# A fixed order for the first four token tiles of a linear-attention and gated-MLP kernel on Trainium2

## The chip, the cores and the metric

The kernel runs on one core of one Trainium2 chip. The metric is the device time of one execution in microseconds (us), as the median of several runs. Before the change it is 2445.57 us, the median of 3 runs (2445.08 to 2446.03).

## What is computed

The input x has 2048 tokens of 1024 features, all in float32. The tokens are layer-normalized, and two branches work on the result xn. Branch A is linear attention with 32 heads of 32 features; branch B is a gated MLP with 3584 hidden features. The result is `x + A * silu(B)`.

```python
xn = layernorm(x)                                   # over the 1024 features, eps 1e-5
q, k, v = split_heads(xn @ wqkv)                    # 32 heads of 32
phi = lambda p: concat(softmax(p), softmax(-p))     # p = q @ w_phi or k @ w_phi, per head
kv, z = phi(k).T @ v, sum(phi(k))                   # per head, over all tokens
o = (phi(q) @ kv) / (phi(q) @ z + 1e-6)
A = merge_heads(o) @ wo
B = (sigmoid(xn @ w_gate) * (xn @ w_up)) @ w_down
out = x + A * silu(B)
```

## The kernel before

**Products.** Every large product is computed by Strassen's scheme in the form of Winograd: seven block products (named B11, B21, T2, T3, T4, T1, B22) in place of eight, with sums of blocks ahead of and behind them. To keep float32 accuracy, each operand is split into a high half in a rounded format (ScalarE's cast at L123) and the rest (VectorE's subtraction at L124); `mm3` adds three products, high by high (L128), high by low (L129) and low by high (L130).

**Tokens and weights.** The tokens are worked on in two halves (c = 0, 1) of eight tiles of 128 tokens. For each half the kernel projects to V, K and Q, each in the order B11, B21, T2, T3, T4, T1, B22, and then does the MLP's gate and up products. One block product of a projection runs over four token groups u, and for each over four k blocks with three matrix instructions each, so 12 matrix instructions for a group and 48 for a product. Operands of weights are kept in a ring of eight slots, filled by `prep()` (a cast and a subtraction of 128x1024 elements, for two slots).

**The opening.** A tile is loaded (`x_load`, L150), normalized (`norm`) and transposed by TensorE in two halves of four 128x128 transposes (`transpose`, L192), into one of four banks of PSUM (banks 4 to 7) that are used in turn. The normalization takes statistics on VectorE (two instructions at L160 and one at L161), adds eps (L165, GpSimd for the first half of the tokens), takes a root on ScalarE (L166) and the reciprocal on VectorE (L167), corrects it by five or six small steps on GpSimd (L169 to L174) and applies scale and bias on ScalarE (L176). Group u of B11 and B21 needs tile u, so tiles 0 to 3 are needed first; a transposed tile is split at once for these two (`operand`), and copied to SBUF by ScalarE (L196) for the sums that later blocks need. T2 and all that follows need sums of tiles 0 to 3 with tiles 4 to 7 (`x_sums`, L204). The sums of V's weight blocks (`v_sums`, L255) are made in place on VectorE and GpSimd once the four blocks have landed; those of K and Q follow from folding w_phi into the weights on TensorE (`fold`, L273), copies by ScalarE (L274), four sums on GpSimd (L229 to L232) and stores to DRAM (L224).

**What sets the order.** The program is traced in the order of the Python code. The framework then orders each engine's instructions, and the DMA issues on SP's queue, by a simulated schedule in which what was traced first has priority among what is ready; `tc.high_priority()` raises a block, and `tc.issue_after(ins)` lets a block come behind `ins` on its engine. Each engine then works strictly in that order. The work on the tiles is put between the groups' products by the list `side`, from which `step()` takes one entry behind each group. In the version before, tile 0 comes first with high priority, then all the `prep()` that fits, then the entries tile 1; tiles 2 and 3; tiles 4 and 5; `v_sums`; tiles 6 and 7; folds.

## Time and profile before

| | us |
|---|---|
| median of 3 runs | 2445.57 |
| the profiled execution | 2443.43 |
| its span, from the first to the last instruction | 2441.6 |
| TensorE busy | 2392.8 |
| VectorE busy | 1716.9 |
| ScalarE busy | 1001.9 |
| GpSimd busy | 987.2 |

The profile shows one execution. In it PE is TensorE's matrix work and PEld its weight loads, DVE is VectorE, ACT is ScalarE, POOL is GpSimd and SP is the engine that issues the loads and stores. A row of the timeline gives the start and the duration of an instruction (or of several alike, xN) in us from the span's start, engine, line, what it writes and reads, and, where the engine had been idle, for how long and what ended that. Durations of instructions that follow each other on an engine overlap a little. In a table by stages each engine has its busy time and its count of instructions; the granted clock of TensorE is a share of full speed.

### The profile page before, as it was taken

The numbers are of one execution on the slowest core, as the hardware profiler recorded it, in microseconds if no ns is written. First come the engines' busy times: TensorE is split into PE (matmuls) and PEld (weight loads), VectorE is DVE, ScalarE is ACT, GpSimd is POOL, SyncE is SP. The second block draws the span as 40 slices with busy tenths as digits, with TensorE's granted clock in tenths as the row PEclk, the third lists the DMA queues.
The fourth block names the chain that finished last, engine by engine and source line by source line (L and its number), as shares of the span: only waits on it lengthen the run. The fifth ranks groups of instructions, "written<-read, shape, count | busy, mean of one in ns | idle before, by whom it ended". The sixth has DMA issues, their size and how long they took to land.

```text
span 2441.6 us, 31984 instructions
## 1 busy us (share of the span) xinstructions
PE 2392.8 (98%) x11076; PEld 1986.7 (81%) x11076; DVE 1716.9 (70%) x2247; ACT 1001.9 (41%) x1495; POOL 987.2 (40%) x665
## 2 busy tenths in 40 slices
PE   7999999999999999999999999999999999998998
PEld 6888888888888878888888888788888888877886
DVE  6533577777776678548858888647889998765554
ACT  6432244544444344323433444423443334454332
POOL 5520146566565400004545453543333335314554
PEclk8999999999999999999999999999999999999999
DMA  7874567777776665457888887896666766755553
GB/s 280 279 255 157 195 226 261 255 257 271 263 276 242 245 216 174 172 203 249 292 301 284 275 316 257 278 339 216 217 231 219 254 218 238 236 197 191 182 182 128
DMA packets 231507, 581.61 MB, mean 238 GB/s; under 512 B 30385, under 2 KB 30385, under 8 KB 226737
## 3 DMA queue, kind: packets, MB, share of 16 engines
q1 hardware_dynamic: 231344, 579.57, 68.7%
q8 instruction: 87, 1.43, 0.2%
q14 instruction: 76, 0.61, 0.1%
HBM read 353.76 MB, written 225.71 MB: 237 GB/s over the span
## 4 chain that ended last, share of the span: by engine, by line
PE 77%; DMA 7%; DVE 6%; issue 4%; POOL 4%; ACT 2%; SPq 0%; ACTq 0%; POOLq 0%; DVEq 0%
PE bank L128 25%; PE bank L130 25%; PE bank L129 25%; DVE x L124 1%; DMA fc<-wf_d 1%; DMA w<-ws_d 1%; PE bank L448 1%; DMA fa<-w_down 1%; PE bank L627 1%; DVE w L124 1%; DMA fb<-w_down 1%; DVE p L124 1%; DMA fb<-wo 1%; ACT x L123 1%; DMA fc<-xo_d 0%
## 5 line engine op out<-in xcount | busy, mean ns | idle before, releaser
L128 PE MATMUL bank<-x,w 128*128 128x512 f32 x2352 | 912.7, 390 | 5.1 <-DVE fb L833 3.1
L129 PE MATMUL bank<-x,w 128*128 128x512 f32 x2352 | 915.9, 389 | 0.5 <-DVE x L124 0.4
L130 PE MATMUL bank<-x,w 128*128 128x512 f32 x2352 | 906.7, 389 | 0.0
L123 ACT CAST w<-fa 128x512 fp32r<-128x512 f32 (+1 forms) x444 | 308.2, 698 | 560.3 <-PE bank L129 335.8
L124 DVE TENSOR_TENSOR w<-fa,w 128x512 fp32r<-128x512 f32 (+1 forms) x444 | 434.8, 984 | 140.7 <-ACT w L123 134.1
L128 PEld LDWEIGHTS bank<-x,w 128*128 128x128 f32 x2352 | 441.6, 188 | 98.6 <-DVE fb L833 4.4
L130 PEld LDWEIGHTS bank<-x,w 128*128 128x128 f32 x2352 | 441.6, 188 | 91.9 <-DVE w L124 0.4
L129 PEld LDWEIGHTS bank<-x,w 128*128 128x128 f32 x2352 | 441.7, 188 | 91.2 <-DVE x L124 1.2
L128 PE MATMUL bank<-w,x 128*128 128x512 f32 x708 | 279.2, 394 | 3.7 <-ACT fb L384 2.1
L130 PE MATMUL bank<-w,x 128*128 128x512 f32 x708 | 278.5, 394 | 1.8 <-DVE x L124 1.8
L129 PE MATMUL bank<-w,x 128*128 128x512 f32 x708 | 277.9, 393 | 0.0
L841 POOL TENSOR_TENSOR fc<-fc 128x512 f32<-128x512 f32 x27 | 43.6, 1615 | 298.9 <-DVE fc L840 286.8
L128 PEld LDWEIGHTS bank<-w,x 128*128 128x128 f32 x708 | 134.0, 189 | 31.8 <-ACT fb L384 2.5
L130 PEld LDWEIGHTS bank<-w,x 128*128 128x128 f32 x708 | 133.8, 189 | 30.0 <-DVE x L124 2.5
L129 PEld LDWEIGHTS bank<-w,x 128*128 128x128 f32 x708 | 134.0, 189 | 27.2 <-DVE w L124 0.2
L577 POOL TENSOR_TENSOR fc<-fc 128x1024 f32<-128x1024 f32 x32 | 81.4, 2543 | 178.3 <-ACT fc L413 123.1
L841 POOL TENSOR_TENSOR fb<-fb,fc 128x512 f32<-128x512 f32 x57 | 91.2, 1600 | 130.7 <-DVE fc L840 107.3
L317 POOL TENSOR_TENSOR fb<-fa 128x512 f32<-128x512 f32 x28 | 36.7, 1309 | 248.2 <-DMA fa<-w_gu 133.7
L124 DVE TENSOR_TENSOR w<-fb,w 128x512 fp32r<-128x512 f32 (+1 forms) x114 | 106.0, 929 | 39.2 <-ACT w L123 37.7
L123 ACT CAST w<-fb 128x512 fp32r<-128x512 f32 (+1 forms) x114 | 71.4, 627 | 133.6 <-PE bank L129 103.8
L124 DVE TENSOR_TENSOR x<-fa,x 128x512 fp32r<-128x512 f32 x112 | 111.1, 993 | 15.6 <-ACT x L123 15.3
L840 DVE TENSOR_TENSOR fc<-fc,bank 128x512 f32<-128x512 f32 x84 | 57.3, 683 | 89.8 <-PE bank L130 75.8
(250 smaller groups left out, 3312.2 us busy)
## 6 DMA issues: line engine op xcount, KB each, us to landing
ws_d<-w SPq DMA_DIRECT2D x112, 512.0 KB, 3.9
w<-ws_d SPq DMA_DIRECT2D x112, 512.0 KB, 5.4
fa<-w_gu SPq DMA_DIRECT2D x84, 512.0 KB, 4.2
fa<-h_d SPq DMA_DIRECT2D x84, 512.0 KB, 4.1
fa<-wf_d SPq DMA_DIRECT2D x32, 1024.0 KB, 5.3
h_d<-fc SPq DMA_DIRECT2D x120, 256.0 KB, 4.0
fc<-e_d SPq DMA_DIRECT2D x48, 512.0 KB, 3.9
fc<-qkv_d SPq DMA_DIRECT2D x80, 256.0 KB, 4.2
```

Of the source, the lines that this page charges most:

```text
L123: nc.scalar.copy(o[0], src)
L124: return nc.vector.tensor_sub(o[1], src, o[0].bitcast(F32))
L128: nc.tensor.matmul(o, a[0], b[0], start=first, stop=False, **kw)
L129: nc.tensor.matmul(o, a[0], b[1], start=False, stop=False, **kw)
L130: nc.tensor.matmul(o, a[1], b[0], start=False, stop=last, **kw)
L317: nc.gpsimd.tensor_add(s1, a21, a22)
L448: nc.tensor.matmul(kvb[g // 2][:, g % 2 * 256:g % 2 * 256 + 256], v[:, g].rearrange("p a f -> p (a f)"), ph[:, g].rearrange("p a f -> p (a ...
L577: nc.gpsimd.tensor_mul(ez, e, zb)
L627: nc.tensor.transpose(ps[:, j * P:(j + 1) * P], e[:, k * P:(k + 1) * P], ident)
L840: v = nc.vector.tensor_add(b, u2 if q == 3 else u1, bank)
L841: nc.gpsimd.tensor_mul(g, g, b)
```

## The change

It touches the opening alone. The 28 transposes of the identity that keep TensorE at work before the first data become 36. Small steps of the normalization of the first half's tiles go from GpSimd to VectorE, with the last two in one instruction; the second half's tiles had theirs there already. Tile 1 is loaded ahead of the first block of wv, which comes in two pieces of 512 KB. The function `first_tiles` writes down the order for tiles 0 to 3 in four parts: the first runs ahead of all products, and the three others behind groups 0, 1 and 2 of B11. `in_order` then ties every TensorE, VectorE and ScalarE instruction traced from the warm-up to the end of the part behind group 3 to the one traced before it on its engine. Within that, the statistics and scales of a tile are traced ahead of the splits of the tile before; the copies of a transposed tile to SBUF are put off (`kept`, `keep_two`) until after the next tile's normalization; and the four `prep()` calls for B11 and B21 stand in parts one, three and four. `v_sums` and the tiles 4 to 7 come behind the last ordered instruction of VectorE, the tiles also behind that of ScalarE, and `v_sums` is now traced ahead of tiles 4 and 5. The loads of tile 6, tile 7 and the last two blocks of wv are traced behind the transposes of tile 0 and tile 1.

```diff
--- before.py
+++ after.py
@@ -1,5 +1,5 @@
 from collections import deque
-from contextlib import ExitStack
+from contextlib import ExitStack, contextmanager
 
 import concourse.bass as bass
 import concourse.tile as tile
@@ -100,7 +100,7 @@
     block("fb", 43, 4, F32)
     block("fc", 47, 8, F32)
     NW = 8
-    WARM = 28
+    WARM = 36
 
     banks = [psum.tile([P, HB], F32, name=f"bank{i}") for i in range(8)]
 
@@ -144,36 +144,59 @@
     XO = {B11: 16, T2: 12, T3: 0, B21: 20, T1: 8, T4: 24, B22: 4}
     tps = Ring(banks[4:])
 
-    last_norm, last_chain = [], []
+    last_chain = []
 
     def x_load(t, slot):
         nc.sync.dma_start(whole(slot), x[t * P:(t + 1) * P, :])
         return whole(slot)
 
-    def norm(tiles, xs):
-        n = len(tiles)
+    @contextmanager
+    def in_order(*engines):
+
+        traced = nc.cur_bb.bb.instructions
+        last, before = traced[-1], {}
+        yield before
+        start = next(k for k in reversed(range(len(traced))) if traced[k] is last) + 1
+        for i in traced[start:]:
+            if i.engine in engines:
+                if i.engine in before:
+                    tc.add_manual_dep(i, before[i.engine].name,
+                                      mybir.DependencyInfo(mybir.DependencyClass.NoSync, mybir.DependencyReason.DATA),
+                                      reason="in_order")
+                before[i.engine] = i
+
+    def stats(tiles, xs):
         st = small.tile([P, 2, 2, 6], F32, name=f"bn{tiles[0]}", tag="bn")
         mv = small.tile([P, 2, 2], F32, name=f"mv{tiles[0]}", tag="mv")
-        ws = small.tile([P, 4, 2], F32, name=f"lnw{tiles[0]}", tag="lnw")
         for i, xt in enumerate(xs):
             for a in range(2):
                 nc.vector.bn_stats(st[:, i, a], xt[:, a * HB:(a + 1) * HB])
             nc.vector.bn_aggr(mv[:, :, i], st[:, i])
+        return mv
+
+    def scales(tiles, mv):
+
+        n = len(tiles)
+        ws = small.tile([P, 4, 2], F32, name=f"lnw{tiles[0]}", tag="lnw")
         v, r, a, b = [ws[:, q, :n] for q in range(4)]
-
-        eng = nc.gpsimd if tiles[0] < CTT else nc.vector
-        eng.tensor_scalar_add(v, mv[:, 1, :n], EPS_LN)
+        nc.vector.tensor_scalar_add(v, mv[:, 1, :n], EPS_LN)
         nc.scalar.activation(a, v, AF.Sqrt)
         nc.vector.reciprocal(r, a)
 
-        eng.tensor_mul(a, r, r)
-        eng.tensor_mul(a, a, v)
-        eng.tensor_scalar(b, a, -0.5, 1.5, op0=ALU.mult, op1=ALU.add)
-        eng.tensor_mul(r, r, b)
-        eng.tensor_mul(b, mv[:, 0, :n], r)
-        last_chain[:] = [eng.tensor_scalar(b, b, -1.0, None, op0=ALU.mult).ins]
+        nc.vector.tensor_mul(a, r, r)
+        nc.vector.tensor_mul(a, a, v)
+        nc.vector.tensor_scalar(b, a, -0.5, 1.5, op0=ALU.mult, op1=ALU.add)
+        nc.vector.tensor_mul(r, r, b)
+        last_chain[:] = [nc.vector.scalar_tensor_tensor(b, mv[:, 0, :n], -1.0, r, op0=ALU.mult, op1=ALU.mult).ins]
+        return r, b
+
+    def normalized(xt, r, b, i=0):
+        nc.scalar.activation(xt, xt, AF.Identity, bias=b[:, i:i + 1], scale=r[:, i:i + 1])
+
+    def norm(tiles, xs):
+        r, b = scales(tiles, stats(tiles, xs))
         for i, xt in enumerate(xs):
-            last_norm[:] = [nc.scalar.activation(xt, xt, AF.Identity, bias=b[:, i:i + 1], scale=r[:, i:i + 1]).ins]
+            normalized(xt, r, b, i)
 
     def operand(c, i, u, b):
 
@@ -183,7 +206,7 @@
         else:
             nc.sync.dma_start(xo_d[i, :, u], b)
 
-    def transpose(t, xt, dst):
+    def transpose(t, xt, dst, kept=None):
 
         c, th, u = t // CTT, t % CTT // 4, t % 4
         for q in range(2):
@@ -193,6 +216,10 @@
             i = {(0, 0): B11, (1, 0): B21, (1, 1): B22}.get((q, th))
             if c == 0 and th == 0:
                 operand(c, i, u, tp)
+            if kept is not None:
+                kept.append((dst[q], tp))
+                yield
+                continue
             nc.scalar.copy(dst[q], tp)
             if c and i is not None:
                 operand(c, i, u, dst[q])
@@ -495,7 +522,7 @@
         xt = x_load(t, 52)
         norm([t], [xt])
         th, u = t % CTT // 4, t % 4
-        transpose(t, xt, halves(53 + th))
+        list(transpose(t, xt, halves(53 + th)))
         if th:
             x_sums(t // CTT, u, halves(53), halves(54))
 
@@ -684,8 +711,10 @@
     xts = [x_load(0, XS[0])]
     phraw = whole(47)[:, :KT * DH].rearrange("p (g f) -> p g f", f=DH)
     nc.sync.dma_start(phraw, w_phi.rearrange("(g p) f -> p g f", p=P))
-    v_load(0)
-    xts += [x_load(t, XS[t]) for t in range(1, 4)]
+    xts.append(x_load(1, XS[1]))
+    for h in range(2):
+        nc.sync.dma_start(slots[39 + h], v_block(0, 0)[:, 2 * h:2 * h + 2])
+    xts += [x_load(t, XS[t]) for t in range(2, 4)]
     v_load(1)
     xts += [x_load(t, XS[t]) for t in range(4, 6)]
 
@@ -693,16 +722,11 @@
         norm(tiles, [xts[t] for t in tiles])
         for t in tiles:
             if t < 4:
-                transpose(t, xts[t], first[t])
+                list(transpose(t, xts[t], first[t]))
             else:
                 b = b12s.next(), b22s[t - 4]
-                transpose(t, xts[t], b)
+                list(transpose(t, xts[t], b))
                 x_sums(0, t - 4, first[t - 4], b)
-            if t < 2:
-                xts.append(x_load(t + 6, XS[t + 6]))
-            if t == 1:
-                v_load(2)
-                v_load(3)
 
     def x_rest():
         for i, name, src in ((B22, "x1", b22s), (T1, "x2", [b[0] for b in first]), (T4, "x6", [b[1] for b in first])):
@@ -712,31 +736,89 @@
         fraw.items = halves(43, 54)
 
 
-    for n in range(WARM):
-        nc.tensor.transpose(banks[3][:, n % 4 * P:(n % 4 + 1) * P], ident, ident)
-    with tc.high_priority():
-        x_tiles(0)
-    with tc.issue_after(last_norm[0]):
-        while prep():
-            pass
     one = whole(44)[:, :P]
     nc.gpsimd.memset(one, 1.0)
     nc.scalar.copy(ones, one)
     nc.gpsimd.memset(bd, 0.0)
+    FIRST = mybir.EngineType.PE, mybir.EngineType.DVE, mybir.EngineType.Activation
+    kept = []
+
+    def tile_of(t):
+
+        yield from transpose(t, xts[t], first[t], kept)
 
     def phi_blocks():
-        with tc.issue_after(last_chain[0]):
-            for j in range(4):
-                nc.gpsimd.tensor_copy(bd[j * DH:(j + 1) * DH, :, j * DH:(j + 1) * DH], phraw[j * DH:(j + 1) * DH])
+        for j in range(4):
+            nc.gpsimd.tensor_copy(bd[j * DH:(j + 1) * DH, :, j * DH:(j + 1) * DH], phraw[j * DH:(j + 1) * DH])
+
+    def first_tiles():
+
+        for n in range(WARM):
+            nc.tensor.transpose(banks[3][:, n % 4 * P:(n % 4 + 1) * P], ident, ident)
+        normalized(xts[0], *scales((0,), stats((0,), xts[:1])))
+        rb = scales((1,), stats((1,), xts[1:2]))
+        parts = tile_of(0)
+        prep()
+        next(parts)
+        prep()
+        next(parts)
+        normalized(xts[1], *rb)
+        xts.append(x_load(6, XS[6]))
+        yield
+        mv = stats((2, 3), xts[2:4])
+        parts = tile_of(1)
+        next(parts)
+        rb = scales((2, 3), mv)
+        next(parts)
+        normalized(xts[2], *rb, 0)
+        keep_two()
+        xts.append(x_load(7, XS[7]))
+        v_load(2)
+        v_load(3)
+        yield
+        parts = tile_of(2)
+        next(parts)
+        next(parts)
+        normalized(xts[3], *rb, 1)
+        prep()
+        keep_two()
+        yield
+        parts = tile_of(3)
+        next(parts)
+        next(parts)
+        prep()
+        keep_two()
+        phi_blocks()
+        yield
+
+    def keep_two():
+        for _ in range(2):
+            o, tp = kept.pop(0)
+            nc.scalar.copy(o, tp)
+
+    FIRST_STEPS = first_tiles()
 
     def todo(f, *a):
         side.append(lambda: f(*a))
 
-    todo(x_tiles, 1)
-    todo(lambda: (x_tiles(2, 3), phi_blocks()))
-    todo(x_tiles, 4, 5)
-    todo(v_sums)
-    todo(x_tiles, 6, 7)
+    first_order = in_order(*FIRST)
+    first_last = first_order.__enter__()
+    next(FIRST_STEPS)
+    for _ in range(3):
+        todo(next, FIRST_STEPS)
+
+    def first_end():
+        keep_two()
+        first_order.__exit__(None, None, None)
+        with tc.issue_after(first_last[mybir.EngineType.DVE]):
+            v_sums()
+
+    def later_tiles(*tiles):
+        with tc.issue_after(first_last[mybir.EngineType.DVE]), tc.issue_after(first_last[mybir.EngineType.Activation]):
+            x_tiles(*tiles)
+    todo(first_end)
+    todo(later_tiles, 4, 5)
+    todo(later_tiles, 6, 7)
     for k in range(4):
         todo(fold, K, k)
     todo(x_rest)
```

## Prediction

> **What bounds the kernel now.** I read the page first, then busy time by stages, then TensorE's waits, then the instructions in order of time.
>
> ```profile
> span 2441.6 us, 31984 instructions
> ...
> PE 2392.8 (98%) x11076; PEld 1986.7 (81%) x11076; DVE 1716.9 (70%) x2247; ACT 1001.9 (41%) x1495; POOL 987.2 (40%) x665
> ```
>
> TensorE (PE) is busy for 2392.8 of 2441.6 us, so 48.8 us is all its idle time. A change to the opening can save only what PE loses there, idle or at half clock. By stages (window; PE, PEld, DVE, ACT, POOL busy; granted clock; DMA share; GB/s):
>
> ```profile
> 9.97:22.16 12.19, 7.49 (x21) 4.89 (x21) 12.09 (x21) 7.25 (x12) 3.61 (x8) 0.58 1.04 395
> 22.16:44.04 21.88, 21.88 (x108) 18.23 (x109) 14.70 (x22) 15.96 (x28) 20.30 (x28) 1.00 0.83 322
> 44.04:53.18 9.14, 5.09 (x34) 4.49 (x34) 3.94 (x3) 8.12 (x11) 2.59 (x2) 0.90 0.39 141
> 53.18:75.40 22.22, 21.16 (x127) 18.19 (x126) 21.86 (x23) 12.68 (x23) 15.04 (x10) 0.97 0.56 176
> 75.40:82.04 6.64, 4.49 (x23) 3.90 (x23) 1.66 (x2) 2.23 (x4) 6.41 (x5) 0.74 0.96 361
> 82.04:200.00 117.96, 117.39 (x595) 99.27 (x594) 47.69 (x55) 40.08 (x57) 34.30 (x25) 1.00 0.74 252
> 200.00:2441.00 2241.00, 2209.37 (x10148) 1832.00 (x10146) 1613.22 (x2120) 911.18 (x1360) 901.78 (x574) 1.00 0.69 236
> ```
>
> From 82.04 on PE is full (117.39 of 117.96): whatever is won before then should reach the end. Before it there are three losses: 9.97 to 22.16 (4.70 idle, clock 0.58, DVE full), 44.04 to 53.18 (4.05 idle) and 75.40 to 82.04 (2.15 idle, clock 0.74). PE's waits in the first 150 us (total, times, longest) name them:
>
> ```profile
> PE bank L192 <- ACT x L176: 4.7, 2, 2.6
> PE bank L192 <- ACT x L196: 4.0, 1, 4.0
> PE bank L273 <- ACT w L123: 2.0, 1, 2.0
> PE bank L130 <- DVE x L124: 1.8, 1, 1.8
> ```
>
> The first and fourth belong to tiles 0 and 1: transposes waiting for the normalization, a product for the low half of its operand. The second is tiles 6 and 7, whose transposes need the banks that ScalarE copies out at L196. Only the first and fourth lie in what the change orders by hand.
>
> **The change, part by part.** The rows (start, duration):
>
> ```profile
> 1.46 5.93 PE L716 MATMUL bank<-ident 128*128 128x128 f32 x28 [1.46 <-POOL ident masks.py:199]
> ...
> 5.99 0.21 DVE L161 BATCH_NORM_AGGREGATE mv<-bn 128x2 f32<-128x12 f32 x1
> ...
> 6.56 0.20 ACT L166 ACTIVATE lnw<-lnw 128x1 f32<-128x1 f32 x1 [2.94 <-POOL lnw L165]
> ...
> 8.68 1.24 ACT L176 ACTIVATE x<-x,lnw 128x1024 f32<-128x1024 f32 x1 [1.91 <-POOL lnw L174]
> 9.82 1.98 ACT L123 CAST w<-fa 128x1024 fp32r<-128x1024 f32 x2
> 9.92 1.29 DVE L160 BATCH_NORM_STATS2 bn<-x 128x6 f32<-128x512 f32 x2 [2.96 <-DMA x<-x]
> ...
> 9.97 1.64 PE L192 MATMUL bank<-ident,x 128*128 128x128 f32 x8 [2.58 <-ACT x L176]
> ...
> 11.12 1.21 DVE L124 TENSOR_TENSOR w<-fa,w 128x1024 fp32r<-128x1024 f32 x1
> 11.70 1.06 ACT L123 CAST x<-bank 128x512 fp32r<-128x512 f32 x2
> ...
> 14.64 0.68 DVE L124 TENSOR_TENSOR x<-bank,x 128x512 fp32r<-128x512 f32 x1
> ...
> 15.37 0.80 PE L130 MATMUL bank<-w,x 128*128 128x512 f32 x1 [1.82 <-DVE x L124]
> ...
> 22.16 1.10 PE L192 MATMUL bank<-ident,x 128*128 128x128 f32 x8 [2.15 <-ACT x L176]
> ...
> 27.90 0.39 PE L128 MATMUL bank<-w,x 128*128 128x512 f32 x1
> 28.13 0.39 PE L129 MATMUL bank<-w,x 128*128 128x512 f32 x1
> ```
>
> The chain between statistics and normalization moves from POOL to DVE; its later rows on DVE, in the second half, give its price:
>
> ```profile
> 364.99 1.29 POOL L318 TENSOR_TENSOR fb<-fb,fa 128x512 f32<-128x512 f32 x1
> 365.15 0.15 DVE L171 TENSOR_SCALAR lnw<-lnw 128x1 f32<-128x1 f32 x1
> 365.34 0.96 DVE L172 TENSOR_TENSOR lnw<-lnw 128x1 f32<-128x1 f32 x1
> ```
>
> A step costs about 0.2 us from start to start, but the two-input one at 365.34 ran until POOL's 1.29 us instruction was over. So 0.2 us is the price with POOL idle, up to one POOL instruction more otherwise.
>
> Tile 0: the statistics end at 6.20; add 0.18, root 0.23, then the reciprocal and five steps, 1.2: normalization starts at 7.8 in place of 8.68. It ends at 9.04. The 36 warm-up transposes take 0.21 us each at first and half of that at full clock, so they end between 8.2 and 9.1; they lie under the wait and cost nothing. Tile 0's transposes start at 9.1 (before: 9.97).
>
> Tile 1's load goes ahead of the 1 MB of wv: at 395 GB/s that is 2.65 us, so it lands at 7.3 at the latest, not 9.92. DVE now does statistics and chain of tile 1 (7.8 + 1.29 + 0.2, add, root, 1.2) before any split: 10.9. ScalarE in order: root to 9.7, weight cast to 10.7, operand cast to 11.2, then 12.2, 12.7, and the normalization of tile 1 to 13.9. DVE in order: weight half to 12.1, operand half 12.75, then 13.9 and 14.5. The third kind of product (L130) can begin at 12.75, in place of 15.37; the last five wait for 13.9, and token group 0 is done at 13.9 + 5 x 0.227 = 15.05 (before: 20.01).
>
> Now the order itself costs something. DVE takes the statistics of tiles 2 and 3 (four of 0.6, two of 0.2: to 17.4) before the low half of tile 1's operand, 18.1. Tile 1's transposes run at 15.05 to 16.0, then L130 waits until 18.1, and group 1 ends ten products later at 20.4. Tile 2 is normalized when the chain is through (19.8) until 21.0; its transposes need the two banks whose copies are put off until then (0.55 each, 21.55 and 22.1); operand halves 22.7 and 23.35, group 2 done at 25.65. ScalarE then normalizes tile 3, casts a weight and copies two banks: 26.5; transposes to 27.0, halves 27.8, group 3 done at 30.1.
>
> What PE has done by then, against now:
>
> ```profile
> 28.59 1.91 PE L192 MATMUL bank<-ident,x 128*128 128x128 f32 x16
> ...
> 44.04 2.22 PE L192 MATMUL bank<-ident,fc 128*128 128x128 f32 x16
> ```
>
> Now PE has 12 products by 20.01, 24 more by 28.6, sixteen transposes to 30.5, and the other 60 of B11 and B21 until 44.04: it fills the wait for tiles 2 and 3 with B21. With the change it has 48 by 30.1 and the next 48, at 0.227, by 41.0. The gain in this part is therefore 44.04 - 41.0 = **3.0 us**, not the 5 us of group 0.
>
> The later loads: tile 7 waits for tile 1's transposes (16.0), and v_load(2) and (3) may queue behind it on SP. 2 MB from 16.0 at 395 GB/s is 21.3, or 23.2 behind the earlier bytes; the sums that read them start after 30.1, so 7 us of cover hide it. ScalarE's 0.55 us copies are put off, not added. POOL's four phi copies come free to run early.
>
> **Tiles 4 to 7.** Here the trace shows no equivalent, so I bound it.
>
> ```profile
> 24.80 2.50 DVE L255 TENSOR_TENSOR p<-fb,p 128x1024 f32<-128x1024 f32 x2
> ...
> 36.85 2.41 POOL L255 TENSOR_TENSOR fa<-fa 128x1024 f32<-128x1024 f32 x1
> ...
> 42.74 2.38 ACT L176 ACTIVATE fc<-fc,lnw 128x1024 f32<-128x1024 f32 x2 [0.69 <-POOL lnw L174]
> ...
> 49.64 2.52 ACT L196 COPY x<-bank 128x512 f32<-128x512 f32 x5
> ...
> 51.69 2.35 DVE L204 TENSOR_TENSOR x<-x 128x512 f32<-128x512 f32 x2 [1.18 <-ACT x L196]
> ```
>
> v_sums now waits for DVE's last ordered split (30.1) and is traced ahead of tiles 4 and 5: DVE's four take 5.0 (24.80 and its like), to 35.0, then the statistics of tiles 4 and 5, 2.9, to 37.9; POOL's four, at 2.41, run from 35.0 to 44.7. The chain of tiles 4 and 5 thus meets POOL. Without a collision it ends at 39.5; if its two-input steps wait for one POOL instruction each, when POOL is through, 45.0; now the normalization starts at 42.74. Tiles 6 and 7 need statistics (2.9) and chain (1.6) after that, 44.0 to 49.5, then 2.5 for two normalizations and 1.0 for transposes: the last one ends between 47.5 and 53.0 (now 53.18). The sums of x for tile 4 follow its normalization by some 4 us (2.5, a transpose, copies) and can start at 44 to 49 in place of 51.69. DVE is full from there to 75.4 (21.86 of 22.22), so this stage moves with its start: it ends 2.7 to 7 us earlier. I take the late end, about 3, since POOL's rows stand right beside the chain. It hands on the 3.0 us already won and adds nothing; the wait of 4 us stays, in another place. Earlier sums and folds also meet nothing new on DMA, whose share is 0.56 there.
>
> **The clock.** The granted clock follows PE's idle time:
>
> ```profile
> 7.00:8.00 1.00, 0.39 (x4) 0.15 (x2) 0.00 (x0) 0.00 (x0) 0.71 (x4) 1.00 1.06 414
> ...
> 51.33:54.70 3.37, 3.37 (x17) 3.26 (x16) 2.92 (x3) 2.06 (x5) 1.56 (x2) 0.50 0.01 3
> ```
>
> Half clock for 3.4 us costs 1.7 us where PE is full. In the ordered opening PE mostly waits for DVE, so half clock there would stretch products into waits: 0 to 1 us. The Trainium skill (TensorE: Matmul & The Clock Gate, Part 4: PE-mode transpose) says that transposes do not count as activity for the clock; by that, eight more would not warm anything, and tile 0's would keep the 1.64 us of 9.97 instead of 1.10. The trace speaks against it: nothing but transposes had run when four fitted into 0.39 us after 7.0. By the rule the time would be 0.5 us longer.
>
> **Sum.** The profiled execution took 2443.43 us, 1.83 more than its span, and lies 2.1 under the median 2445.57. Minus 3.0 it would be 2440.4; the median becomes **2442.6**. That is 0.12% less, inside the 0.2% that a measurement of this kernel can tell from no change.
>
> **Rivals.** (1) The gain stays at 2 to 4.5 us: forecast, 2441 to 2444. (2) Tiles 4 to 7 also gain. Without collisions, and with ScalarE's copies ahead of the casts, the 4.0 us wait shrinks to 1 and its half clock (1.7) goes: 3.0 + 3.0 + 1.7 = 7.7, or 2437.9; a second 2 us from 75.4 would make 2436. For it: norm chains no longer queue behind POOL's sums. Against: DVE is full and now carries them. (3) Slower: the chain on DVE locks with POOL. The Trainium skill (SBUF — State Buffer, Who interferes with whom) says that a VectorE instruction with two SBUF inputs and a GpSimd one that reads SBUF block each other whole; the rows at 364.99 and 365.34 agree. If tiles 6 and 7 meet it too (two more steps, each behind one of POOL's 2.41 us: 4.8 on 53.0), their transposes end at 57.8, 4.6 behind now, and half clock adds 1.7: 6.3 us slower, 2451.9. It decides when tile 7's last transpose ends after 53.2. (4) The order of everything later is worked out anew from the shifted start: 31.6 us of PE's idle time lie after 200 us (2241.00 less 2209.37), and a few of them may move either way. I give that 2 us on each case. (5) The order isn't kept or hardly differs: then 2445.6; the edges name each engine, so little speaks for it.
>
> **Chances.** Forecast 0.50, (2) 0.30, (3) 0.13, (5) 0.07. Faster than 2440.7 is (2) with little of (1): 0.30. Slower than 2450.5 is most of (3): 0.09. Within: 0.61. The likeliest case alone spans 2440 to 2445; the range runs from (2)'s 2437 to halfway into (3), 2448.5.
>
> **What would show it.** Right: tile 0's normalization at 7.8, group 0 done near 15, an L130 wait of 2 us near 16 to 18, B21 done at 41, then a PE gap of several us before tiles 4 to 7. Wrong: B21 before group 3 on PE; tiles 4 and 5 normalized before 40; or waits after 200 us that differ by more than 3 us.

## The result, and the profile after

The changed kernel takes 2454.22 us (median of 6 runs, 2450.82 to 2455.62) against 2445.78 us (median of 6 runs, 2440.37 to 2450.75) before. The ratio is 1.0031, with a 95% interval of 1.0019 to 1.0043: slower, with the whole interval above 1. The prediction of 2442.6 us had the wrong sign, and the time lies above its range.

The page of the changed kernel, in the profiled execution of 2454.54 us:

```profile
span 2452.8 us, 31986 instructions
...
PE 2395.5 (98%) x11084; PEld 1988.2 (81%) x11084; DVE 1721.3 (70%) x2269; ACT 1003.2 (41%) x1495; POOL 973.4 (40%) x630
```

The span is 11.2 us longer. TensorE is idle for 57.3 us of it (48.8 before), and busy for 2.7 us more. Two windows say where. The first 200 us, of the kernel before and then of the changed one (columns as in the prediction's stages):

```profile
0.00:200.00 200.00, 183.43 (x930) 154.66 (x931) 103.65 (x128) 90.69 (x136) 85.45 (x91) 0.96 0.75 260
```

```profile
0.00:200.00 200.00, 174.67 (x896) 146.88 (x897) 109.10 (x153) 88.50 (x134) 72.75 (x56) 0.95 0.73 251
```

In the same 200 us TensorE has done 8.76 us less. After 200 us it is idle for 31.1 us in this profile (2252.00 less 2220.86 in the window from 200 to 2452) and was for 31.6 before. So the loss is made in the opening. By stages of the changed kernel:

```profile
8.27:20.27 12.00, 8.85 (x40) 6.01 (x40) 10.46 (x29) 7.73 (x12) 0.00 (x0) 1.00 1.04 402
20.27:40.29 20.02, 18.96 (x88) 15.02 (x88) 14.89 (x23) 13.54 (x23) 1.89 (x1) 1.00 0.62 239
40.29:54.95 14.66, 0.01 (x1) 0.01 (x1) 13.45 (x18) 5.01 (x8) 10.10 (x4) 0.64 0.60 229
54.95:68.22 13.27, 10.41 (x59) 8.83 (x59) 7.92 (x8) 11.27 (x19) 6.03 (x5) 0.76 0.49 158
68.22:82.00 13.78, 13.78 (x73) 12.22 (x74) 11.73 (x13) 5.78 (x11) 7.69 (x6) 0.87 0.49 157
```

The first two rows are what the change was made for: 4.2 us of idle time up to 40.29, where the products of B11 and B21 end (44.04 before). The third row eats all of it: 14.66 us in which TensorE does nothing, while VectorE is busy for 13.45 and GpSimd for 10.10. TensorE's longest wait in the first 150 us names the place (total, times, longest):

```profile
PE bank L215 <- ACT fc L194: 14.7, 1, 14.7
```

L215 is a transpose and L194 the normalization (L192 and L176 before): the first transpose of tile 4 waits for tile 4 to be normalized. Before, the one large wait there was 4.0 us, for a bank to be copied out. The timeline of VectorE, GpSimd and the two ends of the wait:

```profile
29.92 2.35 DVE L282 TENSOR_TENSOR p<-fb,p 128x1024 f32<-128x1024 f32 x2
...
32.19 2.47 DVE L173 BATCH_NORM_STATS2 bn<-fc 128x6 f32<-128x512 f32 x4
...
34.58 2.46 DVE L173 BATCH_NORM_STATS2 bn<-x 128x6 f32<-128x512 f32 x4
...
36.94 2.35 DVE L282 TENSOR_TENSOR fb<-fa,fb 128x1024 f32<-128x1024 f32 x2
...
38.40 6.41 POOL L282 TENSOR_TENSOR fa<-p,fa 128x1024 f32<-128x1024 f32 x2 [31.42 <-DVE fb L282]
...
40.05 2.56 DVE L124 TENSOR_TENSOR w<-fb,w 128x1024 fp32r<-128x1024 f32 x1 [0.42 <-ACT w L123]
...
42.53 2.37 DVE L182 TENSOR_SCALAR lnw<-mv 128x2 f32<-128x2 f32 x2
44.77 5.62 POOL L282 TENSOR_TENSOR fa<-fa 128x1024 f32<-128x1024 f32 x2
44.82 3.38 DVE L124 TENSOR_TENSOR w<-fb,w 128x1024 fp32r<-128x1024 f32 x1
...
48.12 3.35 DVE L124 TENSOR_TENSOR w<-fa,w 128x1024 fp32r<-128x1024 f32 x1
51.40 0.21 DVE L184 RECIPROCAL lnw<-lnw 128x2 f32<-128x2 f32 x2
...
52.05 1.22 DVE L124 TENSOR_TENSOR w<-fa,w 128x1024 fp32r<-128x1024 f32 x1
...
53.65 2.37 ACT L194 ACTIVATE fc<-fc,lnw 128x1024 f32<-128x1024 f32 x2 [7.55 <-DVE lnw L190]
...
54.95 1.33 PE L215 MATMUL bank<-ident,fc 128*128 128x128 f32 x5 [14.66 <-ACT fc L194]
```

Read it from GpSimd's row. Its four sums of V's weights (L282) wait, by its note, for VectorE's second pair of sums (`fb`, 36.94), run from 38.40 to 50.39, and ran from 28.72 to 39.3 before. Beside them stand four instructions L124 on `w`: the splits of the weights for T2 and T3. The last of them, at 52.05 with GpSimd through, takes 1.22 us; the three beside GpSimd take 2.56, 3.38 and 3.35, and a pair of tiny `TENSOR_SCALAR` takes 2.37. Their ends (42.61, 44.90, 48.20, 51.47) follow those of GpSimd's four sums (41.5, 44.8, 47.1, 50.4): the two engines take turns, and each of these instructions of VectorE comes through after a sum has ended (of the pair, the first took 2.30 us). Below I call this the lock. Against 1.22 for a split and 0.2 for the pair this costs 1.34 + 2.17 + 2.16 + 2.13 = 7.8 us, and the chain of tiles 4 to 7 (reciprocals at 51.40) stands behind it in VectorE's queue.

To compare the runs I use one measure beside the waits: when TensorE starts the n-th product of the kind L128, minus the same in the kernel before. The 32nd is the last of B11 and B21 in the order of before (at 43.27 us there), the 34th lies in T2 (58.91), and from the 130th on (155.95) the difference stays the same until the 400th at least. All from one profiled execution each:

| kernel | 4th | 32nd | 34th | 130th | time ratio to before, 95% interval |
|---|---|---|---|---|---|
| the changed kernel | -4.2 | -3.8 | +11.6 | +9.4 | 1.0031 (1.0019 to 1.0043) |
| e1_pool_chain | -2.8 | -3.1 | +11.9 | +10.8 | 1.0047 (1.0032 to 1.0062) |
| e2_sums_between | -2.9 | -3.2 | +9.0 | +8.8 | 1.0036 (1.0023 to 1.0049) |
| e3_chain_ordered | -2.9 | -3.1 | +7.3 | +8.4 | 1.0039 (1.0026 to 1.0052) |
| e6_splits_behind | -3.2 | -3.5 | +5.4 | +5.8 | 1.0026 (1.0016 to 1.0036) |
| e8_no_pool_sums | -3.4 | -3.7 | +0.3 | +0.8 | 1.0018 (1.0008 to 1.0027) |
| e7_sums_early | -3.4 | -3.3 | +2.3 | +1.8 | 1.0030 (1.0017 to 1.0043) |
| e5_no_order | -0.7 | +1.3 | -2.3 | -2.5 | 0.9996 (0.9987 to 1.0006) |
| e4_before_dve | -0.7 | +6.3 | -0.4 | +1.0 | 1.0012 (1.0001 to 1.0022) |
| e9_chain_slots | -3.2 | -1.7 | +4.9 | +5.8 | 1.0019 (1.0010 to 1.0027) |
| e10_order_two | -3.0 | +11.2 | +0.8 | +9.6 | 1.0043 (1.0031 to 1.0055) |
| e11_order_one | +0.1 | +5.1 | -2.7 | -1.3 | 1.0001 (0.9992 to 1.0010) |
| e12_norm_slots | -4.1 | -2.5 | -0.4 | +1.3 | 1.0014 (1.0004 to 1.0023) |

In e4, e5, e10 and e11 some of B21's products come behind transposes of tiles 4 to 7, so there the 32nd is late without a loss, and the 130th is the one to compare. A ratio and a position may differ by a few us: e7 stands at +1.8 at the 130th product and at +6.3 at the 3300th.

### The profile page after: what moved, and what is told of

The parts are those of the page before. It is cut to its first block, busy times and chain, and to the rows that moved or that the text cites. A ratio compares the mean times of both kernels' runs of the same rounds, so it can differ in the third digit from the quotient of the medians.

```text
span 2452.8 us, 31986 instructions
## 1 busy us (share of the span) xinstructions
PE 2395.5 (98%) x11084; PEld 1988.2 (81%) x11084; DVE 1721.3 (70%) x2269; ACT 1003.2 (41%) x1495; POOL 973.4 (40%) x630
## 4 chain that ended last, share of the span: by engine, by line
PE 80%; DVE 8%; DMA 5%; issue 2%; ACT 2%; POOL 2%; SPq 0%; ACTq 0%; DVEq 0%; POOLq 0%
PE bank L128 26%; PE bank L130 26%; PE bank L129 26%; DVE w L124 2%; PE bank L475 1%; DVE x L124 1%; DMA w<-ws_d 1%; PE bank L654 1%; DVE p L124 1%; PE bank L300 1%; DMA fc<-wf_d 1%; DMA fa<-w_down 1%; DMA fb<-w_down 0%; DVE bn L173 0%; DVE fc L438 0%
## 5 line engine op out<-in xcount | busy, mean ns | idle before, releaser
L128 PE MATMUL bank<-x,w 128*128 128x512 f32 x2352 | 911.8, 390 | 6.1 <-DVE fb L915 2.6
L130 PE MATMUL bank<-x,w 128*128 128x512 f32 x2352 | 904.9, 390 | 0.0
L124 DVE TENSOR_TENSOR w<-fa,w 128x512 fp32r<-128x512 f32 (+1 forms) x444 | 435.3, 985 | 135.3 <-ACT w L123 126.3
L128 PEld LDWEIGHTS bank<-x,w 128*128 128x128 f32 x2352 | 441.4, 188 | 101.2 <-DVE fb L915 4.0
L130 PEld LDWEIGHTS bank<-x,w 128*128 128x128 f32 x2352 | 442.0, 188 | 92.4 <-DVE w L124 0.4
L128 PE MATMUL bank<-w,x 128*128 128x512 f32 x708 | 276.9, 392 | 2.6 <-ACT x L123 1.5
L130 PE MATMUL bank<-w,x 128*128 128x512 f32 x708 | 277.1, 392 | 0.7 <-DVE x L124 0.6
L128 PEld LDWEIGHTS bank<-w,x 128*128 128x128 f32 x708 | 133.4, 188 | 30.6 <-ACT x L123 2.2
L130 PEld LDWEIGHTS bank<-w,x 128*128 128x128 f32 x708 | 133.3, 188 | 29.0 <-DVE x L124 1.9
L124 DVE TENSOR_TENSOR w<-fb,w 128x512 fp32r<-128x512 f32 (+1 forms) x114 | 109.3, 959 | 31.0 <-ACT w L123 26.1
L124 DVE TENSOR_TENSOR x<-fa,x 128x512 fp32r<-128x512 f32 x112 | 111.7, 998 | 20.6 <-ACT x L123 20.6
```

The lines of the kernel that those rows point to most:

```text
L124: return nc.vector.tensor_sub(o[1], src, o[0].bitcast(F32))
L128: nc.tensor.matmul(o, a[0], b[0], start=first, stop=False, **kw)
L130: nc.tensor.matmul(o, a[1], b[0], start=False, stop=last, **kw)
```

## The experiments

The readings to tell apart: that the chain of tiles 4 to 7 itself collides with GpSimd now that it runs on VectorE; that it only queues behind the four splits; that the sums of V's weights are in the way because they are traced ahead of tiles 4 and 5; and that GpSimd's sums, begun 10 us later than before, hold up whatever two-input work VectorE has beside them. Line numbers move by a few in each kernel: the transposes are L215 in the changed kernel, L220 in e1, L211 in e5, and GpSimd's sums L282, L287 and L278.

### The small steps of tiles 4 to 7 back on GpSimd

```diff
-        nc.vector.tensor_scalar_add(v, mv[:, 1, :n], EPS_LN)
+        eng = nc.gpsimd if tiles[0] in (4, 6) else nc.vector
+        eng.tensor_scalar_add(v, mv[:, 1, :n], EPS_LN)
...
-        nc.vector.tensor_mul(a, r, r)
+        eng.tensor_mul(a, r, r)
...
```

> The changed kernel with the small steps of tiles 4 to 7 back on GpSimd, all else as changed. Theory Q (queue: in the changed kernel the reciprocal and the small steps of tiles 4 to 7 stand on VectorE behind three of the four 128x1024 weight splits, which GpSimd's sums stretch from 1.2 to 2.6 to 3.4 us): the reciprocals stay on VectorE behind the same splits, so TensorE's gap ahead of tile 4's transposes stays at 12 to 17 us and the time within 3 us of the changed kernel's. Theory C (collision: the two-input small steps themselves lock with GpSimd, as rival 3 of the prediction had it): with the steps on GpSimd, the gap shrinks to 5 to 9 us and the time falls by 5 to 8 us. Theory O (the fixed order and the later sums hold VectorE until 30 us, so the tiles' statistics are late): no change.

Measured: 2456.92 us, ratio 1.0047. The wait grew to 15.5 us. VectorE's part and GpSimd's part of the timeline of e1:

```profile
46.51 2.35 DVE L124 TENSOR_TENSOR w<-fa,w 128x1024 fp32r<-128x1024 f32 x2
48.78 0.21 DVE L185 RECIPROCAL lnw<-lnw 128x2 f32<-128x2 f32 x2
```

```profile
47.76 5.59 POOL L287 TENSOR_TENSOR fa<-fa 128x1024 f32<-128x1024 f32 x2
53.31 0.34 POOL L187 TENSOR_TENSOR lnw<-lnw 128x2 f32<-128x2 f32 x2
```

The reciprocals still stand behind the splits (48.78), and then GpSimd's own steps stand behind its last two sums (53.31). So the move of the small steps to VectorE, taken alone, is not what costs the 14.66 us.

### The sums of V's weights traced behind tiles 4 and 5

```diff
         first_order.__exit__(None, None, None)
+
+    def sums_after():
         with tc.issue_after(first_last[mybir.EngineType.DVE]):
             v_sums()
...
     todo(later_tiles, 4, 5)
+    todo(sums_after)
```

> The changed kernel with the sums of V's weight blocks traced behind tiles 4 and 5, as before the change; all else as changed. Theory O: the statistics of tiles 4 and 5 come before the sums, and tiles 4 and 5 are transposed by 45 us in place of 55; the time falls by 5 us or more. Theory Q: statistics were done by 37 us anyway and only the small steps were late; they still stand behind the weight splits on VectorE, so the gap stays over 10 us and the time within 3 us of the changed kernel's.

Measured: 2453.3 us, ratio 1.0036; the wait is 14.7 us, as in the changed kernel. (T2's weights are read ahead of their sums here, so the time is read for the opening alone.) Tiles 4 and 5 are normalized at 54.3 instead of 53.65, and GpSimd's sums run from 40.3 to 53.7. So tracing the sums behind tiles 4 and 5 does not take the wait away. It moves GpSimd's sums by 2 us only, and they still lie beside VectorE's two-input work.

### The chain of tiles 4 to 7 inside the fixed order, ahead of the sums

```diff
...
         keep_two()
+        for a in (4, 6):
+            later_rb[a] = scales((a, a + 1), stats((a, a + 1), xts[a:a + 2]))
         first_order.__exit__(None, None, None)
```

> The changed kernel with the statistics and small steps of tiles 4 to 7 written into the end of the fixed order, ahead of the sums of V's weight blocks and of all weight splits for T2 and T3. Theory Q: the chain ends on VectorE by 38 us with GpSimd idle, tiles 4 and 5 are normalized by 40 to 41 us, TensorE's gap falls from 14.7 to under 2 us, and the time is 8 to 14 us below the changed kernel's, 2440 to 2446. Theory O: it makes the sums and T2's weights 8 us later still, TensorE only waits at T2 in place of tile 4, and the time is not below the changed kernel's by more than 3 us.

Measured: 2453.43 us, ratio 1.0039. The longest wait at these transposes fell to 2.1 us, tiles 4 and 5 were normalized at 39.4, and nothing was won: T2's first product now waits 8.16 us. From the timeline of e3, engine by engine:

```profile
53.77 6.60 POOL L282 TENSOR_TENSOR fa<-fa 128x1024 f32<-128x1024 f32 x2
```

```profile
54.81 3.36 DVE L124 TENSOR_TENSOR w<-fa,w 128x1024 fp32r<-128x1024 f32 x1
58.09 2.82 DVE L124 TENSOR_TENSOR x<-x,x 128x512 fp32r<-128x512 f32 x1
```

```profile
63.22 0.79 PE L128 MATMUL bank<-w,x 128*128 128x512 f32 x1 [8.16 <-ACT x L123]
```

With tiles 4 to 7 out of the way the same lock takes the next work in line: a weight split (3.36 for 1.22) and a split of x (2.82 for 0.68), beside GpSimd's sums, which now run until 60.4. That the chain only queued behind the splits is true of the changed kernel and still no explanation of the time.

### The four weight splits behind the chain of tiles 4 to 7

```diff
-            while prep():
-                pass
+            if n == 1:
+                with tc.issue_after(last_chain[0]):
+                    while prep():
+                        pass
+            elif n:
+                while prep():
+                    pass
```

> The changed kernel with the four weight splits for T2 and T3 held on VectorE (and their casts in the order that follows) until the small steps of tiles 4 to 7 are through; the sums of V's weight blocks stay where they are, so GpSimd's sums run beside the small steps. Theory Q: the small steps end at 42 to 45 us in place of 53.7, the gap falls to 4 to 6 us and the time by 6 to 10 us. Theory C: the eight two-input steps each wait for GpSimd's 2.4 us sums until these are over at about 49 us, the gap stays over 9 us and the time falls by less than 4 us.

Measured: 2451.09 us, ratio 1.0026; the wait is 9.9 us. Now the small steps themselves stand beside GpSimd's sums (38.71 to 48.7). VectorE's timeline:

```profile
39.86 2.08 DVE L182 TENSOR_SCALAR lnw<-mv 128x2 f32<-128x2 f32 x2
...
42.51 1.73 DVE L186 TENSOR_TENSOR lnw<-lnw 128x2 f32<-128x2 f32 x2
44.20 2.33 DVE L187 TENSOR_TENSOR lnw<-lnw 128x2 f32<-128x2 f32 x2
46.49 2.34 DVE L188 TENSOR_SCALAR lnw<-lnw 128x2 f32<-128x2 f32 x2
48.80 0.23 DVE L189 TENSOR_TENSOR lnw<-lnw 128x2 f32<-128x2 f32 x2
```

Each pair of 0.23 us waits for one sum, four pairs for four sums. The collision of the chain that the prediction priced exists, but only where the chain meets the sums; in the changed kernel the splits met them in its place. After these four, what they have in common is GpSimd's sums, wherever the others are put; that VectorE simply has too much work ahead of the chain is not ruled out yet.

### GpSimd's four sums left out

```diff
-                               (pool, 0, 3, 0, "subtract"), (pool, 1, 1, 0, "subtract")):
+                               )[:2]:
```

> The changed kernel without GpSimd's four sums of V's weight blocks (T2's and B22's weights are then not the sums they should be, so its time is read for the opening alone). Theory L (lock: GpSimd's sums, moved from 28.7 to 38.4 us, stretch every two-input instruction of VectorE beside them, in the changed kernel by 7.9 us ahead of the reciprocals): nothing is stretched, the reciprocals come at 43 to 45 us in place of 51.4, the gap ahead of tile 4 falls from 14.7 to 5 to 8 us, and the time by 6 to 10 us. Theory S (start: VectorE is simply busy until 30 us, and the work behind it is late without any collision): the gap stays over 11 us and the time within 3 us of the changed kernel's.

T2's and B22's weights are then not the sums, so the time is read for the opening alone. Measured: 2447.45 us against 2443.09, ratio 1.0018. The wait at tile 4 is 6.38 us; in VectorE's rows the splits take 1.17 to 1.22 again; one of them, and TensorE's wait:

```profile
41.88 1.17 DVE L124 TENSOR_TENSOR w<-fb,w 128x1024 fp32r<-128x1024 f32 x1
```

```profile
46.80 3.67 PE L215 MATMUL bank<-ident,fc 128*128 128x128 f32 x16 [6.38 <-ACT fc L194]
```

Tiles 4 and 5 are normalized at 45.51, 8.1 us earlier than in the changed kernel; the rows above gave 7.8 us for the lock. TensorE stands at +0.8 instead of +9.4 at the 130th product. The lock is thereby shown as the cause of some 8 us of the wait in the opening. (The splits no longer need GpSimd's results either, but in the changed kernel VectorE had no idle time between 40.05 and 53.7, so no wait for these was in it.) The measured time shows less of it: 1.0018 against 1.0031 is 1.3 thousandths, or 3.2 us, and the two intervals overlap. What the lock leaves matters too: without a single sum on GpSimd, T2 starts no earlier than before (+0.3). The 3.7 us won by then are given back at tile 4, whose chain comes behind the sums and splits of VectorE.

### The sums of V's weights started earlier

VectorE's two pairs go into the fixed order, ahead of the third and the fourth split for B21; GpSimd's come right behind. All sums are made.

```diff
...
         normalized(xts[3], *rb, 1)
+        v_sums("add")
         prep()
...
+        v_sums("sub")
         prep()
...
-        with tc.issue_after(first_last[mybir.EngineType.DVE]):
-            v_sums()
+        v_sums("pool")
```

> The changed kernel with VectorE's sums of V's weight blocks inside the fixed order (two ahead of the third weight split, two ahead of the fourth), so that GpSimd's four can start near 31 us in place of 38.4; all the sums are made. Theory L: GpSimd is through by 41 to 43 us in place of 50.4, the small steps of tiles 4 to 7 end at 45 to 48 in place of 53.7, the gap falls to 6 to 9 us and the time by 4 to 8 us. Theory S: VectorE's total ahead of the small steps is the same, so the gap stays over 12 us and the time within 3 us.

Measured: 2449.48 us, ratio 1.0030. The wait at tile 4 fell to 7.8 us and TensorE to +1.8 at the 130th product, with GpSimd's sums at 30.15 to 41.4. The ratio does not show that gain: its interval is nearly that of the changed kernel, and by its profile 4.5 us were lost again after the 400th product.

### The same text without the order's edges

```diff
             if i.engine in engines:
-                if i.engine in before:
-                    tc.add_manual_dep(i, before[i.engine].name,
...
                 before[i.engine] = i
```

> The changed kernel without the edges that tie the instructions of TensorE, VectorE and ScalarE in the opening to the traced order; the tracing, the loads, the 36 transposes and the steps on VectorE stay as changed. If the edges are what brings TensorE's products forward, group 0 of B11 ends at 17 to 20 us in place of 15.2 and B21 at 42 to 44 in place of 40.3. Theory L with the edges as what moved the sums: the sums on VectorE come at 25 to 32 us again, GpSimd's end by 40, the gap falls under 8 us, and the time is 4 to 8 us below the changed kernel's, 2446 to 2450. If the move of the steps to VectorE does the harm without the edges, the time stays over 2451.

Measured: 2442.21 us against 2443.09, ratio 0.9996, better than the 2446 to 2450 that I had expected. Loads, warm-up, VectorE's chain and the late copies are all as in the changed kernel; without the edges nothing is lost, and TensorE stands at -2.5 at the 130th product. GpSimd's and VectorE's timelines of e5:

```profile
27.53 5.54 POOL L278 TENSOR_TENSOR fa<-p,fa 128x1024 f32<-128x1024 f32 x2 [20.53 <-ACT fc L404]
```

```profile
28.34 1.88 DVE L124 TENSOR_TENSOR x<-bank,x 128x512 fp32r<-128x512 f32 x3
...
33.37 2.07 DVE L182 TENSOR_TENSOR lnw<-lnw 128x2 f32<-128x2 f32 x1
35.37 2.45 DVE L178 TENSOR_SCALAR lnw<-mv 128x2 f32<-128x2 f32 x1
```

GpSimd's sums begin at 27.53 again. The instruction behind which `v_sums` is put is the last weight split that was traced; without edges VectorE makes it at 17.97, and in the changed kernel, held behind the work on tile 3, at 28.78. Beside the sums of e5 stand mostly splits that read a PSUM bank (0.63 each) and statistics (0.64 each), which are not stretched. Two small steps of tiles 4 to 7 are, and the wait at tile 4 is still only 0.7 us.

### The small steps on VectorE, in the kernel before

```diff
-        eng = nc.gpsimd if tiles[0] < CTT else nc.vector
+        eng = nc.vector
```

> The kernel before with one part of the change alone: the small steps of all tiles of the first half on VectorE. If the move by itself does the harm (the steps lock with GpSimd's sums), tiles 4 to 7 are normalized 3 to 8 us later than in the kernel before and the time is 3 to 7 us above it. If it needs the fixed order and the later sums, the time is within 3 us of the kernel before.

Measured: 2445.74 us against 2443.09, ratio 1.0012, and +1.0 at the 130th product; tiles 4 and 5 are normalized at 39.29, earlier than before (42.74). In the opening this part alone makes about a ninth of the loss (1.0 of 9.4 us); its ratio, with an interval up to 1.0022, does not exclude more.

### The chain of tiles 4 to 7 in VectorE's idle time

From e7, the statistics of tiles 4 and 5 go behind tile 1's splits, where VectorE had been idle (one of its gaps ends at 22.45 in the changed kernel), and those of 6 and 7 behind the last split for B21.

```diff
...
         normalized(xts[2], *rb, 0)
+        mv = stats((4, 5), xts[4:6])
...
+        later_rb[4] = scales((4, 5), mv)
         v_sums("add")
...
+        later_rb[6] = scales((6, 7), stats((6, 7), xts[6:8]))
```

> This is e7_sums_early (VectorE's sums of V's weights inside the fixed order, GpSimd's from about 30 us) with the statistics and scales of tiles 4 and 5 put into the order where VectorE stood idle in the changed kernel (19.8 to 22.5 us, behind tile 1's splits), and those of tiles 6 and 7 behind the last split for B21. Theory L (GpSimd's late sums lock the VectorE work that gates tiles 4 to 7): tiles 4 and 5 are then normalized at about 31 to 35 us, TensorE's wait at the first transpose of tile 4 (14.66 us in the changed kernel, 7.80 in e7) falls below 1 us, and what is left is a wait of 0 to 4 us for tiles 6 and 7, whose scales still stand beside GpSimd's sums of about 30 to 41 us. TensorE stands between 3 us ahead of the kernel before and 2 us behind it from the 130th product on; the ratio is 0.998 to 1.002. Rival M (the wait only moves on, as in e3_chain_ordered, since all of this work still lies beside GpSimd's sums): waits of 6 us or more appear between 40 and 66 us in other places, at the sums of x or at tiles 6 and 7, and the ratio stays at 1.002 to 1.004.

Measured: 2449.27 us against 2444.7, ratio 1.0019, +5.8 at the 130th product, and waits of 6.0 and 3.0 us: nearer to the rival. The scales of tiles 4 and 5 were ready at 25.7 us, yet they were applied only at 47.13. ScalarE's timeline:

```profile
45.13 0.20 ACT L183 ACTIVATE lnw<-lnw 128x2 f32<-128x2 f32 x1 [4.87 <-DVE lnw L182]
...
47.13 2.40 ACT L194 ACTIVATE fc<-fc,lnw 128x1024 f32<-128x1024 f32 x2
```

The root for tiles 6 and 7 (L183) stood in ScalarE's fixed order ahead of them, and waited for a step of VectorE that stood behind two locked splits. A hand-made order carries a lock on one engine into another engine's queue.

### The order closed behind part two

```diff
+    def part_two():
+        next(FIRST_STEPS)
+        first_order.__exit__(None, None, None)
+    todo(part_two)
...
-        with tc.issue_after(first_last[mybir.EngineType.DVE]):
-            v_sums()
+        v_sums()
...
```

> The changed kernel with its fixed order closed behind part two (tiles 0 and 1 and the splits for their two groups); tiles 2 to 7 and the sums of V's weights go where the schedule puts them. Theory L: GpSimd's sums start at 27 to 32 us again, as before and in e5_no_order, TensorE's waits between 39 and 60 us sum to less than 6 us, and the gain of the first part stays: group 0 ends at about 15 us and TensorE stands 1 to 4 us ahead of the kernel before from the 130th product on; the ratio is 0.9980 to 0.9995. Rival M (the early part of the order itself does the harm, by the loads and copies that it moves): GpSimd's sums still start at 36 us or later, the wait at tile 4 stays at 10 us or more, and the ratio stays at 1.002 to 1.004.

Measured: 2456.31 us, ratio 1.0043, and +9.6 at the 130th product. Here the theory fell in the form that I had given it. GpSimd's sums did start at 27.79, as early as before, and the kernel is still slow. VectorE's, GpSimd's and TensorE's rows of e10:

```profile
27.79 5.53 POOL L282 TENSOR_TENSOR fa<-p,fa 128x1024 f32<-128x1024 f32 x2 [21.10 <-DVE lnw L189]
```

```profile
28.67 2.32 DVE L187 TENSOR_TENSOR lnw<-lnw 128x2 f32<-128x2 f32 x1
...
30.99 0.68 DVE L124 TENSOR_TENSOR x<-bank,x 128x512 fp32r<-128x512 f32 x1
```

```profile
31.72 0.80 PE L130 MATMUL bank<-w,x 128*128 128x512 f32 x1 [5.47 <-DVE x L124]
```

The schedule has put small steps of tiles behind VectorE's sums, so they lie beside GpSimd's. One of 0.16 us takes 2.32, and the split that a product of B11 waits for stands behind it in the queue. So an early start of the sums does not save the time; what stands beside them matters. The lock is not all of this wait: VectorE's own sums (four of 1.22 us, from 23.92 to 28.75) stand ahead of that split as well, and the granted clock was 0.50 from 30.2 to 36.9. How the +9.6 divides among the three is not shown.

### The order closed behind part one

```diff
     next(FIRST_STEPS)
+    first_order.__exit__(None, None, None)
     for _ in range(3):
...
```

> The changed kernel with its fixed order closed behind part one (tile 0, tile 1's normalization, the first two weight splits and group 0); all behind it goes where the schedule puts it. VectorE's queue then has the last small step of tiles 2 and 3 behind one pair of the sums of V's weights, and those of tiles 4 and 5 behind both pairs, beside GpSimd's sums. Theory L2 (the harm comes where two-input work of VectorE that gates a tile lies beside GpSimd's sums, wherever these start): GpSimd's sums start at 27 to 30 us; the steps of tiles 2 and 3 are past before them, so the wait at tile 2 is 1 to 3 us (one pair of VectorE's sums, 2.4 us) and not the 5.47 us of e10_order_two; the steps of tiles 4 and 5 are locked, which their slack hides; TensorE stands 3 us ahead to 1 us behind the kernel before from the 130th product on, ratio 0.9985 to 1.0005. Rival M (any fixed part of the order costs what e10 did, 9 us): a wait of 5 us or more at 25 to 32 us, ratio 1.003 or more.

Measured: 2443.63 us against 2443.27, ratio 1.0001, and -1.3 at the 130th product. The mended theory holds in the total and misses a place: the wait at tile 2 is 0.46 us, and another of 3.56 us comes at 35.57, where the steps of tiles 4 and 5, locked for 2.35 and 1.20 us (29.07 and 32.54), stand ahead of a split of x (34.85), with statistics between them. I had thought that their slack would hide them; their neighbours in the queue had none.

### Tiles 4 and 5 normalized early as well

Against e9:

```diff
...
-        v_sums("sub")
         prep()
+        v_sums("sub")
+        for i in range(2):
+            normalized(xts[4 + i], *later_rb[4], i)
```

> This is e9_chain_slots with the scale-and-bias of tiles 4 and 5 on ScalarE put into the fixed order ahead of the root for tiles 6 and 7, which it waited behind until 47.13 us, and with the last split for B21 ahead of the second pair of VectorE's sums. Theory L2: the wait at tile 4 (6.00 us at 42.46 in e9) goes, since tiles 4 and 5 are normalized by 33 us; what stays is a wait of 2 to 6 us between 42 and 54 us for the sums of x, T2's weights or tiles 6 and 7, whose work still lies beside GpSimd's sums of about 31 to 44 us; TensorE stands 2 us ahead to 3 us behind the kernel before from the 130th product on, ratio 0.9985 to 1.0012. Rival M (the wait moves on to T2's first product in full): waits between 42 and 60 us sum to 9 us as in e9 and the ratio stays at 1.0015 to 1.003.

Measured: 2447.75 us against 2443.27, ratio 1.0014, and +1.3 at the 130th product. Tiles 4 and 5 are normalized at 28.72, and the wait at tile 4 is down to 0.61 us. The next one is at the transposes of tiles 6 and 7, which need the banks of tiles 4 and 5:

```profile
49.46 3.68 PE L215 MATMUL bank<-ident,x 128*128 128x128 f32 x16 [5.09 <-ACT x L223]
```

L223 copies a transposed tile out. ScalarE comes to these copies at 48.84, behind the normalization of tiles 6 and 7, whose chain has two steps of 2.13 us beside GpSimd's last sums. The waits from 42 to 60 us sum to 7.2 us (0.61, 5.09 and 1.51), not to the rival's 9; the ratio lies between what the two expected. Of all versions with the whole fixed order this one has the lowest ratio, and it is not faster than the kernel before.

## Why the prediction was wrong

**Up to 40 us it was right, but for one step**:

```profile
7.79 1.24 ACT L194 ACTIVATE x<-x,lnw 128x1024 f32<-128x1024 f32 x1 [1.22 <-DVE lnw L190]
...
9.09 1.09 PE L215 MATMUL bank<-ident,x 128*128 128x128 f32 x8 [0.82 <-ACT x L194]
...
15.01 1.04 PE L215 MATMUL bank<-ident,x 128*128 128x128 f32 x8
...
17.70 0.50 PE L130 MATMUL bank<-w,x 128*128 128x512 f32 x1 [0.63 <-DVE x L124]
...
21.01 1.14 PE L215 MATMUL bank<-ident,x 128*128 128x128 f32 x8 [0.74 <-ACT fc L797]
...
33.53 0.59 ACT L408 COPY fc<-bank 128x512 f32<-128x512 f32 x1 [2.83 <-PE bank L130]
```

Tile 0 is normalized at 7.79 (7.8 forecast) and transposed at 9.09 (9.1); tile 1's transposes start at 15.01 (15.05). The wait at L130 is there and smaller, 0.63 instead of 2 us. Tile 2 is transposed from 21.01 and waits for the copies that were put off, at L797, as said. TensorE is through with B21 at 40.29 (41.0), so the term "44.04 - 41.0 = 3.0 us" measured 3.75. The one step is group 3: it was to be done at 30.1, and its result is copied out at 33.53 (L408 copies B11's results). The order does not tie the products of B21. Seven of their k blocks had started by then, where the forecast let TensorE wait for tile 3, and TensorE was busy without a break from 25.4 to 33.1. "B21 before group 3 on PE" was listed as a sign of being wrong, and it came. It helped, so part of the 0.75 us by which the term beat the forecast is luck. The price of the steps on VectorE (0.2 us each), the 36 warm-up transposes at no cost, and the loads with 7 us of cover all held.

**The step that failed is "Tiles 4 to 7"**, in its sentence "I take the late end, about 3, since POOL's rows stand right beside the chain. It hands on the 3.0 us already won and adds nothing". The last transpose was bounded by 47.5 and 53.0; it came at 60.91. The normalization of tiles 4 and 5 was bounded by 39.5 and 45.0; it came at 53.65. The sign of being right, "a PE gap of several us before tiles 4 to 7", came too, and had no size. Three things in the working of these bounds were wrong:

- The queue was incomplete. It had VectorE's sums, the statistics and the chain. The four weight splits for T2 and T3 were left out; before, they stood in VectorE's idle time (38.49 and 46.09). Alone they take 4.9 us (4 x 1.22).
- The lock was laid on the wrong instructions. I priced the chain's small steps against GpSimd's sums and gave the splits nothing, though they too have two inputs. Three of the splits met the sums, and the four took 10.5 us. The small steps behind them came after the last sum, and only the pair at 42.53 was caught, a `TENSOR_SCALAR` of one input, a kind that I had given no lock at all. My price came from steps of 128x1 in the second half, where the one-input step (365.15) took 0.15 us beside GpSimd.
- The place of the sums was taken as traced. I had GpSimd's from 35.0 to 44.7, at 2.41 each. The schedule put the statistics of tiles 4 to 7 (32.19 to 37.0) between VectorE's two pairs, so they began at 38.40, and with VectorE between them took 12.0 us, until 50.39.

Rival (3) named the mechanism (VectorE locks with GpSimd), the place (tiles 4 to 7), the point from which it decides (a last transpose after 53.2) and a price of 6.3 us; by the medians the loss is 8.4. It had a chance of 0.13, since I took each collision as one short step waiting once, and not as a queue of long instructions that take turns with GpSimd for 12 us. That its price came near the loss is partly luck: it was worked out for small steps of tiles 6 and 7, which are not what was held.

**Beside it.** That the stage behind "moves with its start" held, against the kernel: TensorE is 11.6 us late at the 34th product and still 9.4 at the 130th, and some half clock is in that stage (0.76 and 0.87 in the two rows from 54.95 to 82). The Trainium skill's rule on transposes and the clock (TensorE: Matmul & The Clock Gate, Part 4: PE-mode transpose) would have left tile 0's transposes at 1.64 us; after nothing but transposes they took 1.09 (row 9.09), so the trace does not bear it out. The case that nothing changes (5) is ruled out by the rows above, and (4), a shift after 200 us, by the equal idle time there.

**What is shown and what is not.** That GpSimd's sums cause some 8 us of the wait is shown by leaving them out (e8); that the fixed order puts them in that place, by taking its edges away (e5); that the wait follows whatever stands beside them, by e3, e6 and e11, and with other causes beside it by e10 and e12. How much of the measured time the lock makes is less sure than its share of the wait (e8). Not settled is why the ratios of e7 and e8 stay 2.3 and 1.5 thousandths above what TensorE's position at the 400th product gives. Their profiles lose another 4.5 and 2.6 us from there to the 3300th product. A new order is not the reason: from 158.3 us of the changed kernel on, TensorE, VectorE and ScalarE work in the same order in all three, and the changed kernel loses 2.3 us there. Single runs of the kernel before differ by more than that (2440.37 to 2450.75). No version here beats the kernel before by more than its measurement can tell; the nearest is the changed text without its edges (0.9996).

## What to carry to other kernels

Before an order is fixed by hand, write down for each engine the whole queue behind it, and mark every two-input VectorE instruction (and, as here, every `TENSOR_SCALAR` of more than one element) that will stand beside a long GpSimd one: it costs up to the rest of that one, and all that queues behind it pays. Work of GpSimd belongs where VectorE is idle or reads PSUM, and an earlier first product is worth only as much as the next stage is ready to take. Where a wait ends, look first at what the next wait will be: here the 34th product, in T2, started at 58.9 us before, and at 58.47 at the earliest in the versions with the whole fixed order, so there the up to 4 us won ahead of it had nowhere to go.
